# Retention and a routed expert layer: order of the last routing steps, and two weight halves between VectorE and GpSimd

## The chip, the cores and the metric

The kernel runs on one core of a Trainium2 chip. The metric is the device time of one execution in microseconds (us). The kernel before has a median of 381.22 us over 3 runs (381.2 to 381.51).

## The reference

Inputs are `q`, `k`, `v` of shape (4, 8, 768, 64) and an expert layer with a gate of (512, 8), `w1` of (8, 512, 1024) and `w2` of (8, 1024, 512). First comes a retention, a linear attention whose state decays by a factor per head:

```python
for t in range(S):
    state = gamma * state + einsum('bhd,bhe->bhde', k[:, :, t], v[:, :, t])
    y[:, :, t] = scale * einsum('bhd,bhde->bhe', q[:, :, t], state)
```

Its result, as 3072 tokens of 512 features, goes to eight experts. Each token goes to one:

```python
logits = x @ w_gate
expert_idx = argmax(logits, axis=1)
gate_w = softmax(logits)[arange(N), expert_idx]
for e in range(E):
    xe = x[expert_idx == e]
    out[expert_idx == e] = gate_w * (relu(xe @ w1[e]) @ w2[e])
```

## The kernel before, in words

**Retention.** The tokens are worked in 24 chunks of 128 (4 batches of 6 chunks), two chunks per turn of the loop at L606 (n = 0 to 11, `last` = 11). A turn computes scores, the carried state and the output on TensorE. VectorE takes the output out of PSUM (`evict`, L331), TensorE transposes it (`rows`, L340), and ScalarE copies the rows to SBUF. `logits` and `finish_logits` (L378, L387) multiply the same output with the gate.

**Gating.** The chunks fall into seven groups (L47); the last two, 5 and 6, are chunks 20, 21 and chunks 22, 23. A group goes through `choose` (L417, VectorE: maximum, tie-break and one-hot of the expert, seven instructions for a group of two chunks), `soft` (L436, ScalarE: exponentials), `rank` (L439, TensorE: small matmuls that count the tokens of each expert so far), `slots`, `weights`, `advance` (L450, L483, L456, VectorE) and `label` (L487, two copies on ScalarE). Then GpSimd scatters the rows of the chunk into a DRAM area sorted by expert (`send_apart`, L358); between two such sends it has a `pause`, a small operation on one partition (L199).

**The early expert.** Once 18 chunks are ranked, the kernel knows one expert with many rows and loads 256 of its rows (`fetch_early`). In the last turn they are transposed, and split into a high half (ScalarE, `cut_high`) and a low half (`cut_low`: the first 128 rows on GpSimd, the second on VectorE). All products are made of three matmuls: high by high, low by high, high by low. The expert's work is cut into 32 pieces of 6 matmuls (`early_pieces`, L883): two per block of 128 hidden features, two per block of the second product. Order: hidden 0, hidden 1, result 0, hidden 2, result 1, and so on. After the second piece of a hidden block ScalarE applies relu (L904), and VectorE takes the low half of that (L905). `fill(n)` (L547) emits the next n pieces. They fill TensorE between the gating steps of the last two groups; `FILL` (L46) has the counts. `mark_early` (L536) makes the scatter indices of the early rows for later, in four VectorE instructions.

**Weights.** A quarter of an expert's weights is loaded to `raw` (a ring of two buffers, L125) and split by `split` (L140): ScalarE copies the high part, and the engine that is passed subtracts it for the low part. For the first expert this is done in steps of 512 columns, whose turns stand in `SPLITS` (L60); turn 11 has one, the last step of quarter 1. For the second expert a quarter is split in two halves of 1024 columns; its first quarter is split at the end of `late_block` (L1050), which works the early expert's remaining rows ahead of the loop over the experts 1 to 7 (L1119).

**Order.** Everything around the change is under a manual schedule: each engine runs its instructions in the order in which the program emits them. Behind the last choice stands a chain of small VectorE instructions (L733 to L757) that counts the tokens of each expert, sorts the experts by count and computes pad rows; it leads to the loads of the next experts' rows and weights (L761 to L773).

Of the kernel before, what the change touches and what calls it, by code (L numbers as in the profile page):

```python
# [42 lines left out]
ROW = 4 * SLICE  # L43
MAXB = CMAX32 // 32
WARM = 8
FILL = (1, 3, 4)  # L46
GROUPS = ((0, 6), (6, 6), (12, 4), (16, 2), (18, 2), (20, 2), (22, 2))  # L47
FULL = 18
BEHIND = {3: (0, 1), 4: (2, 3), 5: (4, 5), 6: (6, 7), 7: (10, 11), 8: (12, 13)}
# [10 lines left out]
SPLITS = {n: tuple(next(_ORDER) for _ in range(c)) for n, c in _PIECES.items()}  # L60
# [47 lines left out]
def retention_moe(ctx, tc, front, qkv, w1, w2, first_rows, second_rows, out):  # L108
    nc = tc.nc
# [111 lines left out]
    with ExitStack() as actx:  # L221
# [136 lines left out]
        def send_apart(chunks, between=pause):  # L358
            for i, g in enumerate(chunks):
                if i:  # L360
                    between()
                send_rows(g)
# [24 lines left out]
        def finish_logits(t):  # L387
            i = [n for n, (a, w) in enumerate(GROUPS) if a <= 2 * t < a + w][0]
            a, w = GROUPS[i]
            both = ps_1.tile([P, 2, TW], F32, name="lp", tag="misc")  # L390
            lp, state["spare"] = both[:, 0].rearrange("p (c n e) -> p c n e", c=2, n=NP), both[:, 1]
            for ci in range(2):
                nc.tensor.transpose(out=lp[:, ci].rearrange("t p e -> t (p e)"),
                                    in_=state["LT"][:, ci * C:(ci + 1) * C], identity=ident)
            if w == 2:
                lgs[i] = state["spare"][:, 3 * w * E:4 * w * E].rearrange("p (i e) -> p i e", e=E)
            elif 2 * t == a:
                lgs[i] = gsm.tile([P, w, E], F32, name=f"lg{w}")
            nc.vector.tensor_reduce(out=lgs[i][:, 2 * t - a:2 * t - a + 2, :], axis=AX.X, op=ALU.add,
                                    in_=lp[:, :, :, 0:E].rearrange("t c p e -> t c e p"))  # L400
# [131 lines left out]
        def cut_early():  # L532
            for j, w, eng in first["pieces"]:
                cut_low(nc, eng, *first["x"], first["xt"], j, w)

        def mark_early():  # L536
            xg0 = first["xg"]
            index, weight = slot_marks[0]
            empty = gsm.tile([P, NJ0], F32, name="empty0")
            nc.vector.tensor_tensor(out=empty, in0=k_("slot")[:, 0:NJ0], in1=s0.broadcast_to([P, NJ0]), op=ALU.is_ge)  # L540
            nc.vector.tensor_scalar(out=mask0, in0=empty, scalar1=float(BIG), scalar2=k_("quad"),
                                    op0=ALU.mult, op1=ALU.add)
            nc.vector.scalar_tensor_tensor(out=index[:, 0:NJ0], in0=xg0.bitcast(I32)[:, :, P], scalar=4 * ROWS,
                                           in1=mask0, op0=ALU.bitwise_and, op1=ALU.bitwise_or)
            nc.vector.tensor_copy(out=weight[:, 0:NJ0], in_=xg0[:, :, P + 1:P + 2])

        def fill(n):  # L547
            for _ in range(n):
                fn, a = early.pop(0)
                fn(*a)  # L550
# [49 lines left out]
        last = NCH // 2 - 1  # L600
# [5 lines left out]
        for n in range(last + 1):  # L606
            a, b = 2 * n, 2 * n + 1
            s = gating(chosen[n]) if n in chosen else None
            if s:
                stages[chosen[n]] = s  # L610
            begin(n)
            if n == soon:
                logits(n - 1)
            else:
                if n == 0:
                    output(a)
                carry(n)
            if n > 0:
                if n == last:
                    turn_early()  # L620
                if n != soon:
                    logits(n - 1)
                if n == last:
                    for j, w, _ in first["pieces"]:
                        cut_high(nc, first["x"][0], first["xt"], j, w)
                if n in AMID:
                    send_behind(state["LT"][:, 0:1], AMID[n])
                rows(a - 2, "s0")
                rows(a - 1, "s1")
                finish_logits(n - 1)  # L630
            if n in (6, 7):
                for i in SPLITS[n]:
                    split(0, *i, nc.gpsimd if n == 6 else nc.vector, 1)
            if s and n < last:
                s["choose"]()
            if n == soon:
                carry(n)
            if b % CPB < CPB - 1:
                update(b)
            if s and n < last:  # L640
                s["soft"]()
            if n > 0:
                output(a)
            if n == soon:
                s["rank"]()
            output(b)
            if n == soon:
                for name in ("slots", "weights", "label", "counts"):
                    s[name]()
                nc.vector.tensor_copy(out=filled, in_=full)  # L650
                nc.vector.tensor_scalar(out=s0, in0=full, scalar1=base, scalar2=float(EARLY), op0=ALU.subtract,
                                        op1=ALU.min)
                nc.vector.tensor_tensor(out=start, in0=s0, in1=base, op=ALU.add)
                send_apart(range(FULL - 2, FULL))
                fill_late()
                fetch_early()
            elif s and n < last:
                s["rank"]()
                s["slots"]()
            for g in (a, b):  # L660
                evict(g)
            if n == GROUPS[0][1] // 2:
                s["totals"]()
            if n == last:
                cut_early()
                s["choose"]()
            elif s:
                for name in ("weights", "label")[2 * (n == soon):] + ("advance",):
                    s[name]()
            if n == soon - 1:  # L670
                scale(b + 2)
                scale(a + 4)
            if n in BEHIND:
                send_behind(xTs[n][:, 0, C:C + 1], BEHIND[n], pause if n == soon - 1 else lambda: scale(b + 2))
            if n == 1:
                nc.vector.tensor_scalar(out=run, in0=k_("ebase"), scalar1=1.0 / P, scalar2=None, op0=ALU.mult)
            if n < last:
                if n > 0:
                    update(a + 2)
                if n in AFTER:  # L680
                    pause()
                    send_behind(ubs[(a + 2) % 3][:, 0, 0:1], AFTER[n])
                scores(a + 2)
                if n == 0:
                    update(a + 2)
                scores(b + 2)
            if n == GROUPS[0][1] // 2:
                s["pick"]()
                expert_at[0] = nc.sync.value_load(first_at[0:1, 0:1], min_val=0, max_val=E - 1)
                fetch(0, 0)  # L690
                fill_rows()
                fetch(0, 2)
            if n == 0:
                nc.scalar.copy(out=wgs[:, :, 0:E], in_=k_("gates").rearrange("p (k e) -> p k e", k=NP))
            if n < last:
                if n not in BEHIND:
                    scale(b + 2)
                if n < last - 1 and n != soon - 1:
                    scale(a + 4)
            for i in SPLITS.get(n, ()) if n > 7 else ():  # L700
                split(0, *i, nc.gpsimd, 1)
            for g in (a, b):
                if FIRST <= g < NCH - AHEAD - len(MID):
                    load(g + AHEAD + len(MID))
                if g in fetches:
                    fetch(0, fetches[g])
                for i in LATER.get(g, ()):
                    load(i)
        send_apart(range(FULL, FULL + 2))
        mark_early()  # L710

        s = stages[5]
        fill(FILL[0])
        rows(2 * last, "U", ps_1)
        logits(last)
        rows(2 * last + 1, "s1")
        s["soft"]()
        fill(FILL[1])
        s["rank"]()
        for name in ("slots", "weights", "advance", "label"):  # L720
            s[name]()
        send_apart(range(20, 22))
        finish_logits(last)
        final = gating(6)
        final["choose"]()
        fill(FILL[2])
        final["soft"]()
        final["rank"]()
# [42 lines left out]
        expert_at[2] = place(2)  # L771
        for part in range(3):
            fetch(1, part)  # L773
        for i, pieces in enumerate((4, 3, 3, 2)):
            fill(pieces)
            split(0, 3, i, nc.vector, 1)
# [156 lines left out]
def moe_main(ctx, tc, wparts, fetch, split, xhl1, Z0, ident, buf, xg, fetch_rows, expert_at, held7, mask7, slot_marks, natural, overflow,  # L933
             last_meta, pad_regions, token_index, pause, out):
    nc = tc.nc
# [114 lines left out]
    def late_block():  # L1050
# [48 lines left out]
        turned(1)  # L1099
        prep(2, "low")  # L1100
        prep(3, "high", "low")
        for i in range(2):
            split(1, 0, i, nc.vector)
        marks(1)
        for j in range(-(-NJ0 // 4)):
            weigh(0, j)
# [246 lines left out]
```

## Time and profile before

The profiled execution took 381.39 us; its span, from first to last instruction, is 379.6 us.

| engine | busy us | share of the span |
|---|---|---|
| TensorE matmul (PE) | 372.5 | 98% |
| TensorE weight load (PEld) | 350.5 | 92% |
| VectorE (DVE) | 251.9 | 66% |
| ScalarE (ACT) | 140.6 | 37% |
| GpSimd (POOL) | 262.2 | 69% |

Times in the rows are microseconds from the span's start. L12 is line 12 of the kernel; out<-in are the program's names. Matmuls are pipelined and their ends are modelled, so starts are the better measure. Spans on GpSimd are rough. A bracket at the end of a row says how long the engine was idle before it, and what ended that.

### The profile page before, as it was taken

The page shows a single profiled execution, that of the slowest core. Times are in us where ns is not written, and L with a number is a line of the kernel's source. Part 1 is how long each engine was busy: PE and PEld are TensorE (multiplying, and loading weights), DVE is VectorE, ACT ScalarE, POOL GpSimd, SP SyncE. Part 2 cuts the span into 40 slices and gives each one's busy share as a digit, 9 for nine tenths or more (in the row PEclk, how much of TensorE's full clock was granted, in tenths as well). Part 3 has the DMA queues.
Part 4 walks back from the last instruction along what each step waited for, and adds up shares of the span by engine and source line. Part 5 has one row for each costly group of instructions (what it writes and reads, how often), then busy time and mean ns, then how long its engine had stood idle before and what let it go on. Part 6 is the DMA issues. An engine that isn't in the chain of part 4 may idle for free. (4 is left out here: it accounts for less than half of the span.)

```text
span 379.6 us, 8704 instructions
## 1 busy us (share of the span) xinstructions
PE 372.5 (98%) x3279; PEld 350.5 (92%) x3279; DVE 251.9 (66%) x495; ACT 140.6 (37%) x251; POOL 262.2 (69%) x278
## 2 busy tenths in 40 slices
PE   8999999999999999999999999999999999999994
PEld 5888888888899899999999999999999999999984
DVE  3457857887776785967885777576676667676211
ACT  2222244235532645443540553154235316423100
POOL 3751669988770369507996999499669929886874
PEclk9999999999999999999999999999999999999999
DMA  8999999986249579769655654856557557520102
GB/s 303 417 418 416 418 397 419 415 348 167 94 156 190 209 187 298 247 224 253 215 183 104 217 183 142 182 175 194 144 152 221 180 91 239 185 105 17 43 23 77
DMA packets 42030, 82.05 MB, mean 216 GB/s; under 512 B 4267, under 2 KB 17583, under 8 KB 39536
## 3 DMA queue, kind: packets, MB, share of 16 engines
q1 hardware_dynamic: 36656, 67.67, 54.2%
q0 software_dynamic: 5312, 13.49, 9.9%
q8 instruction: 47, 0.77, 0.9%
q14 instruction: 15, 0.12, 0.1%
HBM read 65.80 MB, written 15.82 MB: 215 GB/s over the span
## 5 line engine op out<-in xcount | busy, mean ns | idle before, releaser
L841 POOL DMA_INDIRECT out<-Z,sidx x88 | 101.7, 1156 | 63.8 <-DVE Z L1044 49.1
L146 DVE TENSOR_TENSOR wlo<-raw,whi 128x1024 fp32r<-128x1024 f32 (+1 forms) x63 | 74.2, 1184 | 17.5 <-ACT whi L145 17.4
L201 POOL TENSOR_TENSOR idle<-cs 1x256 bf16<-1x256 f32 x102 | 80.4, 788 | 2.9
L145 ACT CAST whi<-raw 128x1024 fp32r<-128x1024 f32 (+1 forms) x72 | 67.5, 950 | 8.2 <-DMA raw<-w 8.1
L1201 PE MATMUL py<-hh,whi 128*128 128x392 f32 (+4 forms) x192 | 65.9, 343 | 0.0
L1201 PE MATMUL py<-hl,whi 128*128 128x392 f32 (+4 forms) x192 | 65.9, 343 | 0.0
L1201 PE MATMUL py<-hh,wlo 128*128 128x392 f32 (+4 forms) x192 | 65.9, 343 | 0.0
L1176 ACT ACTIVATE hh<-ph 128x452 fp32r<-128x452 f32 (+6 forms) x56 | 28.4, 506 | 73.6 <-PE ph L1169 73.6
L1169 PE MATMUL ph<-xl,whi 128*128 128x392 f32 (+5 forms) x224 | 48.9, 340 | 0.0
L1169 PE MATMUL ph<-xh,wlo 128*128 128x392 f32 (+5 forms) x224 | 48.9, 340 | 0.0
L1169 PE MATMUL ph<-xh,whi 128*128 128x392 f32 (+5 forms) x224 | 48.8, 340 | 0.0
L1177 DVE SCALAR_TENSOR_TENSOR hl<-ph,hh 128x452 fp32r<-128x452 f32 (+6 forms) x56 | 32.0, 573 | 17.5 <-ACT hh L1176 16.8
L1169 PEld LDWEIGHTS ph<-xh,whi 128*128 128x128 f32 x224 | 40.2, 188 | 0.3
L1169 PEld LDWEIGHTS ph<-xl,whi 128*128 128x128 f32 x224 | 40.2, 188 | 0.1
L1169 PEld LDWEIGHTS ph<-xh,wlo 128*128 128x128 f32 x224 | 40.2, 188 | 0.1
L1201 PEld LDWEIGHTS py<-hl,whi 128*128 128x128 f32 x192 | 36.1, 188 | 0.2
L1201 PEld LDWEIGHTS py<-hh,wlo 128*128 128x128 f32 x192 | 36.1, 188 | 0.2
L1201 PEld LDWEIGHTS py<-hh,whi 128*128 128x128 f32 x192 | 36.0, 188 | 0.2
L863 ACT CAST xh<-buf 128x512 fp32r<-128x512 f32 (+7 forms) x26 | 14.4, 556 | 52.6 <-DVE buf L856 52.5
L280 DVE TENSOR_TENSOR Sb<-sp,cs 128x512 f32<-128x512 f32 x48 | 29.8, 682 | 5.8 <-PE sp L277 5.8
L841 POOL DMA_INDIRECT x_sorted<-xrow,KEY x24 | 25.0, 1040 | 7.1 <-issue 3.9
L1039 DVE STREAM_TRANSPOSE Z<-py 128x416 f32<-128x416 f32 (+3 forms) x24 | 15.0, 624 | 18.7 <-PE py L1201 18.4
(197 smaller groups left out, 555.3 us busy)
## 6 DMA issues: line engine op xcount, KB each, us to landing
raw<-w SPq DMA_DIRECT2D x32, 1024.0 KB, 6.7
qkv_w<-qkv SPq DMA_DIRECT2D x12, 1024.0 KB, 17.5
qkv_t<-qkv SPq DMA_DIRECT2D x7, 1024.0 KB, 16.4
qkv_t<-front SPq DMA_DIRECT2D x7, 512.0 KB, 6.9
buf<-x_sorted SPq DMA_DIRECT2D x12, 211.2 KB, 5.2
x_sorted<-cs SPq DMA_DIRECT2D x7, 260.0 KB, 6.5
buf<-x_sorted SPq DMA_DIRECT2D x8, 195.0 KB, 3.8
out<-Z,sidx POOLq DMA_INDIRECT x88, 2.5
```

The costliest lines, as they stand in the source:

```text
L145: nc.scalar.copy(out=hi[:, h], in_=raw[:, h])
L146: engine.tensor_tensor(out=lo[:, h], in0=raw[:, h], in1=hi[:, h].bitcast(F32), op=ALU.subtract)
L201: nc.gpsimd.tensor_tensor(out=idle[0:1], in0=cs[0:1, 0:PAUSE], in1=cs[0:1, 0:PAUSE], op=ALU.mult)
L280: nc.vector.tensor_tensor(out=Sb[:, r], in0=sps[r], in1=causal.unsqueeze(1).broadcast_to([P, NP, C]), op=ALU.mult)
L841: sc = tc.nc.gpsimd.indirect_dma_start(out=dst, out_offset=bass.IndirectOffsetOnAxis(ap=index, axis=0), in_=rows, in_offset=None, bounds_c ...
L863: nc.scalar.copy(out=xh[:, :, c0:c0 + w], in_=xt[:, :, t0:t0 + w])
L1039: nc.vector.transpose(out=Zs[e][:, 0:nb, k, :], in_=py[:, 0:32 * nb].rearrange("p (j c) -> p j c", c=32))
L1169: nc.tensor.matmul(out=ph[:, :w], lhsT=wparts[e, f // 4][a][:, kd, fo:fo + P], rhs=x[:, kd, :w], start=(n == 0), stop=(n == 3 * KD - 1))
L1176: nc.scalar.activation(out=hh[:, :cap], in_=ph[:, :cap], func=AF.Relu)
L1177: nc.vector.scalar_tensor_tensor(out=hl[:, :cap], in0=ph[:, :cap], scalar=0.0, in1=hh[:, :cap].bitcast(F32), op0=ALU.max, op1=ALU.subtract)
L1201: nc.tensor.matmul(out=py[:, :c], lhsT=a[:, f % 4, k * P:(k + 1) * P], rhs=x[:, :c], **se)
```

## The change

It has five parts. In the last turn of the loop, group 5's `choose` is emitted ahead of the early rows' low half. Group 5's `rank` comes ahead of the second early piece, `label` ahead of `advance`, and `FILL` becomes (1, 1, 2): one piece instead of three lies between the last rows and the last logits' transposes, and two instead of four ahead of the last rank. The four pieces left over are emitted later, behind the loads of the second expert's weights, and `mark_early` moves there too. The weight step of turn 11 goes from GpSimd to VectorE, behind the last `choose`. In `late_block`, the second half of the second expert's first quarter goes from VectorE to GpSimd.

```diff
-FILL = (1, 3, 4)
+FILL = (1, 1, 2)
...
             if n == last:
+                s["choose"]()
                 cut_early()
-                s["choose"]()
...
-            for i in SPLITS.get(n, ()) if n > 7 else ():
+            for i in SPLITS.get(n, ()) if 7 < n < last else ():
                 split(0, *i, nc.gpsimd, 1)
...
         send_apart(range(FULL, FULL + 2))
-        mark_early()
 
         s = stages[5]
         fill(FILL[0])
...
         logits(last)
         rows(2 * last + 1, "s1")
         s["soft"]()
-        fill(FILL[1])
         s["rank"]()
-        for name in ("slots", "weights", "advance", "label"):
+        for name in ("slots", "weights", "label", "advance"):
             s[name]()
         send_apart(range(20, 22))
+        fill(FILL[1])
         finish_logits(last)
         final = gating(6)
         final["choose"]()
+        for i in SPLITS[last]:
+            split(0, *i, nc.vector, 1)
         fill(FILL[2])
         final["soft"]()
         final["rank"]()
...
         for part in range(3):
             fetch(1, part)
+        fill(4)
+        mark_early()
         for i, pieces in enumerate((4, 3, 3, 2)):
             fill(pieces)
             split(0, 3, i, nc.vector, 1)
...
         prep(3, "high", "low")
-        for i in range(2):
-            split(1, 0, i, nc.vector)
+        for i, eng in enumerate((nc.vector, nc.gpsimd)):
+            split(1, 0, i, eng)
         marks(1)
```

## Rows read from the trace of the kernel before

**Rows 1.** Busy time by stretch: PE, PEld, DVE, ACT, POOL; clock; DMA share, GB/s.

```profile
86.00:372.00 286.00, 285.97 (x1797) 278.16 (x1796) 194.53 (x347) 112.57 (x180) 203.51 (x207) 1.00 0.56 167
...
160.00:170.00 10.00, 10.00 (x54) 9.81 (x53) 7.47 (x11) 4.43 (x6) 0.00 (x0) 1.00 0.65 216
```

**Rows 2.** Timeline of TensorE's matmuls: start, us, line, out<-in, count.

```profile
99.05 0.48 PE L896 MATMUL ph<-xh,wlo 128*128 128x256 f32 x2
...
99.83 0.64 PE L896 MATMUL ph<-xh,whi 128*128 128x256 f32 x4
...
101.26 0.18 PE L441 MATMUL pf<-EA,us 128*128 128x16 bf16 x1
...
101.48 0.42 PE L393 MATMUL lp<-cs,LT 128*128 128x128 f32 x2
...
104.54 0.18 PE L441 MATMUL pf<-EA,us 128*128 128x16 bf16 x1
...
134.78 0.92 PE L1169 MATMUL ph<-xh,wlo 128*128 128x420 f32 x4
```

**Rows 3.** Timeline of VectorE.

```profile
97.83 1.27 DVE L870 TENSOR_TENSOR xl<-xt,xh 128x512 fp32r<-128x512 f32 x1
99.03 0.16 DVE L422 TENSOR_REDUCE mx<-lp 128x2 f32<-128x16 f32 x1
...
100.03 0.61 DVE L540 TENSOR_TENSOR empty<-cs,s 128x8 f32<-128x8 f32 x1
...
101.10 0.42 DVE L905 SCALAR_TENSOR_TENSOR hl<-ph,hh 128x256 fp32r<-128x256 f32 x1
101.88 0.42 DVE L905 SCALAR_TENSOR_TENSOR hl<-ph,hh 128x256 fp32r<-128x256 f32 x1 [0.35 <-ACT hh L904]
102.22 0.17 DVE L452 TENSOR_TENSOR rk<-pf,EA 128x16 f32<-128x16 f32 x1
...
102.50 0.16 DVE L484 TENSOR_REDUCE GW<-exs 128x2 f32<-128x18 f32 x1
...
102.85 0.22 DVE L399 TENSOR_REDUCE lp<-lp 128x16 f32<-128x64 f32 x1
...
104.04 0.16 DVE L434 TENSOR_TENSOR sh<-lp,mx 128x16 f32<-128x16 f32 x1
...
105.49 0.17 DVE L452 TENSOR_TENSOR rk<-pf,EA 128x16 f32<-128x16 f32 x1
...
109.83 0.23 DVE L371 TENSOR_SCALAR pads<-ends,cs 128x7 int32<-128x7 f32 x1
...
132.20 2.35 DVE L146 TENSOR_TENSOR wlo<-raw,whi 128x1024 fp32r<-128x1024 f32 x2
...
138.03 1.23 DVE L146 TENSOR_TENSOR wlo<-raw,whi 128x1024 fp32r<-128x1024 f32 x1 [0.31 <-ACT whi L145]
```

**Rows 4.** Timeline of GpSimd.

```profile
97.27 1.29 POOL L146 TENSOR_TENSOR wlo<-raw,whi 128x512 fp32r<-128x512 f32 x1
...
124.14 0.60 POOL L201 TENSOR_TENSOR idle<-cs 1x256 bf16<-1x256 f32 x1
...
138.64 1.07 POOL L201 TENSOR_TENSOR idle<-cs 1x256 bf16<-1x256 f32 x1
```

**Rows 5.** Timeline of ScalarE.

```profile
99.33 0.59 ACT L348 COPY xrow<-tr 128x512 f32<-128x512 f32 x1
100.15 0.22 ACT L437 ACTIVATE exs<-sh 128x16 f32<-128x16 f32 x1 [0.23 <-DVE sh L434]
...
101.46 0.38 ACT L904 ACTIVATE hh<-ph 128x256 fp32r<-128x256 f32 x1 [0.82 <-PE ph L896]
102.90 0.21 ACT L490 COPY xrow<-GW 128x8 f32<-128x8 f32 x1 [1.05 <-DVE GW L485]
...
131.02 2.00 ACT L145 CAST whi<-raw 128x1024 fp32r<-128x1024 f32 x2
```

**Rows 6.** Timeline of TensorE's weight loads.

```profile
134.59 0.76 PEld L1169 LDWEIGHTS ph<-xh,wlo 128*128 128x128 f32 x4
```

## The prediction

> **What bounds the kernel now.** I read the busy shares of the page first, then a table of stretches, then the timelines of the engines around the edit. From 86 to 372 us TensorE is busy for 285.97 of 286.00 us at a granted clock of 1.00; VectorE has 194.53 us of work there, ScalarE 112.57 and GpSimd 203.51 [rows 1]. All edits lie inside this stretch. Nobody else's idle time matters: TensorE does the same matmuls before and after, so a microsecond saved on VectorE buys nothing, and a microsecond for which TensorE must wait is a microsecond of the total. The ends of matmuls are modelled, so I go by starts: six 128x256 matmuls take 0.7 us, two pieces of the early expert 1.43 us (99.83 to 101.26), and no start is late [rows 2]. The question is only where the new order leaves TensorE without operands.
>
> **Choice ahead of the low half, and where group 5 is ranked.** The choice of rows 20 and 21 moves in front of the early rows' low half: it runs from 99.03 to 100.03 now, 1.00 us, and would start at 97.83 [rows 3]. The low half then starts at 98.83. It took 1.27 us, beside GpSimd's weight half of 97.27 (1.29 us) [rows 3, 4]. That half is leaving GpSimd, so I take 0.7 us: VectorE's 128x1024 subtractions take 2.35 us for two [rows 3], 0.6 us per 512 columns. It ends at 99.5 instead of 99.10; the 0.60 us pause between two row sends [rows 4] can push that to 100.1. TensorE ranks group 5 at 99.05, behind the transposes, and the choice is ready by 98.83: no wait. The rank takes 0.22 us (101.26 to 101.48), so the second half of hidden block 0, which needs the low rows from its third matmul on (about 99.6), may wait up to 0.5 us, likely 0.1. It takes 0.78 us (99.05 to 99.83) [rows 2].
>
> **Fewer pieces between lp and the last rank: the main term.** Before, four pieces lie between the transposes of the last logits and the last rank: 101.48 to 104.54, 3.06 us [rows 2]. After, there are two, 1.43 us. Without waits TensorE would reach the last rank at 99.05 + 0.22 + 0.78 + 0.20 (the two transposes: 3.06 less 2 x 1.43) + 1.43 + 0.08 for the first of a group = 101.75 us.
>
> What that rank needs comes later, because both other queues are in program order. ScalarE copies the last rows' transposes until 99.92, then takes exp (0.22 us) to about 100.1 [rows 5]. VectorE then does the weights; the label follows 0.40 us after they start (102.50 to 102.90) [rows 3, 5], so at 100.5. In the new order the label stands ahead of the relu of block 0: two copies 0.1 us apart, and relu runs 100.70 to 101.08 (0.38 us). VectorE's low half of that relu follows 0.04 us later, as 101.88 follows 101.46 + 0.38, and the next instruction 0.34 us after it starts: 101.46 [rows 3, 5]. Only there comes the reduce of the last logits and the last choice: 102.85 to 104.20 before, 1.35 us, so until 102.81 after; with the hand-over 102.85. TensorE would stand from 101.75 to 102.85: **1.1 us**. Bounds: if the low half of the relu didn't hold VectorE, the reduce would follow the transposes at 100.4 and the rank could start at 101.8, a wait of 0.1; with the late low rows everything shifts by 0.4, a wait of 1.5. I take the middle value since each link of it has its own row.
>
> **The weight half moved to VectorE** stands behind the last choice. It costs VectorE about 0.65 us after 102.8, ahead of the low half of block 1, which the second result block needs only about 3 us after the rank. TensorE's cost is 0. It delays the release of its raw buffer to about 103.5, and the load into that buffer stands behind the order of experts, which comes out of VectorE's long chain (105.49 to 109.83 before) [rows 3]. Cost 0; without that cover it would be the 5 us by which the release is late.
>
> **mark_early moved** takes its four instructions (100.03 to 101.10, 1.07 us [rows 3]) from ahead of the gating to behind the pad chain. There they stand between the low halves of blocks 2 and 3. The gating and the chain run about 1.7 us earlier (slots at 103.8 instead of 105.49, pads done at 108.4 instead of 110.06), so block 2's low half is there at 108.8; TensorE wants it 0.26 + 4 x 1.43 = 6.0 us after the rank, at 108.9, and block 3's almost 3 us later. Cost 0, with 0.1 us to spare; if the chain loses more to the pauses, up to 0.4. Scatters of the last rows, pads and loads of rows go out about 1.5 us earlier; since TensorE has no wait for them to shorten [rows 1], they give 0.
>
> **The half of the next expert moved to GpSimd: the second term.** ScalarE has both high halves at 133.02 (131.02 + 2.00) [rows 5]. VectorE does its half from 132.20 to 133.38 [rows 3]. A GpSimd operation that meets one of VectorE's with both inputs in SBUF waits for it: the pause at 138.64 takes 1.07 us beside VectorE's subtraction of 138.03 to 139.26, against 0.60 us alone [rows 3, 4]; in the same way the low half of 97.83 waited for GpSimd. So GpSimd starts in effect at 133.38. Its time for 128x1024 is not in the trace; twice its 128x512 is 2.58 us, VectorE's own is 1.18. By the nearest row, its own, it ends at 135.96. TensorE loads the third of four low weights at 134.59 + 2 x 0.19 = 134.97 [rows 6], for the group that starts at 134.78 [rows 2]. That is 0.99 us late by the full double, 0.8 if half of a fixed share is saved, and nothing at VectorE's speed. I take **0.9 us**, bounds 0 to 1.0. All before it in this block hangs on TensorE's own transposes, so the first wait doesn't widen the slack.
>
> The Trainium skill speaks against this edit: "GPSIMD Engine Reference", section 4.1, sends two-input elementwise work to VectorE, being about twice as slow on GpSimd, and section 3.1 has the ratio 1.96. As an estimate from that page, 1.96 x 1.18 = 2.3 us, the half would end at 135.7 and the wait be 0.7 us. Section 8 names the shared SBUF interfaces with contention for two SBUF inputs, and the trace agrees (1.07 against 0.60 us).
>
> What queues behind this half: the weighing of the first expert's rows on VectorE, which has both inputs in SBUF, starts some 2 us later, and so do the nine scatters behind it; VectorE has room in the next blocks, and GpSimd is empty from 160 to 170 us [rows 1]. The loads of weights behind it start 1.4 us later; they cost 0 while ScalarE is not held beyond its slack.
>
> **Sum.** 1.1 + 0.9 = 2.0 us on the profiled execution's 381.39 us (span 379.6, and 1.8 around it) = 383.4. That run lies 0.17 us above the median of 381.22, so **383.2 us**.
>
> **Rivals.**
> Only one of the two waits comes: GpSimd finishes in time because its 1024 columns cost well under two times 512, or the last choice gets through. For: no row has that size on GpSimd. Against: it has 1.6 us from 133.38 for what would be 2.3 to 2.6. Time 381.22 + 0.9 to 1.1 = 382.2. Chance 0.17.
>
> Not slower: the choice of the last group isn't held. Its place is ScalarE's queue: if relu of block 0 got in ahead of the label, or if the last choice ended by 101.75, the 1.1 us go; with GpSimd done by 134.97, nothing is left. It decides at the start of the last logits' reduce: by 100.4 there is no wait. For: the gating chain as a whole runs 1.7 us earlier. Against: program order on ScalarE and VectorE. Time 381.2 to 381.7. Chance 0.16.
>
> Faster: group changes on TensorE cost about 0.08 us more than the steady pace; if modelled ends hide waits there, five changes give back 0.4, and low rows or pads that come earlier might end one that I can't see. 380.8 or below; against it stands 285.97 of 286.00 [rows 1]. Chance 0.06.
>
> Worse: the long chain loses to pauses, block 2's low half is late too, and weights of the next expert are held up behind the later loads: 0.4 + 0.5 more, 384.1. Chance 0.06.
>
> **How the numbers follow.** My forecast, with both waits, has 0.55; its own range is 382.6 to 383.8. Slower by over 0.2% (0.76 us, about what this kernel's measurement can tell from no change) takes the forecast, the single wait and the worse case: 0.78. Within 0.2% takes the not-slower rival and a small share of the faster one, 0.16; faster is 0.06. The range 381.4 to 383.9 leaves out most of the cases without a wait and the worst one.
>
> **What would show it.** TensorE's table of waits, nearly empty in this stretch now, would have a wait of about 1.1 us at the last rank for VectorE, around 102 us, and one of about 0.9 us at the first hidden block of the second expert for GpSimd, near 136 us; the reduce of the last logits would start near 101.5, and one GpSimd subtraction of 128x1024 would take 2.3 to 2.6 us. A start of the last rank below 102.2 us, or that GpSimd half under 1.7 us, would break a term. TensorE busy without a gap would make the whole wrong.

## The result, and the profile after

The changed kernel takes 384.14 us (median of 7 runs, 383.48 to 385.65) against 381.42 us for the kernel before on the same chip (381.2 to 382.56): a ratio of 1.0066 (95% interval 1.0053 to 1.0079), slower by 2.7 us where 2.0 were forecast, and 0.24 us above the range (381.4 to 383.9). The profiled execution took 384.24 us, 2.85 more than the one before (381.39). The granted clock has no part in it: it is 1.00 in every stretch below, as before.

The windows of the changed kernel answer to [rows 1] (columns as there, two shorter stretches added):

```profile
86.00:374.00 288.00, 286.87 (x1795) 277.78 (x1793) 196.16 (x347) 112.92 (x180) 205.91 (x207) 1.00 0.56 166
...
95.00:105.00 10.00, 9.30 (x108) 8.03 (x103) 7.22 (x31) 5.14 (x15) 8.94 (x9) 1.00 0.32 121
...
134.00:144.00 10.00, 9.56 (x50) 8.83 (x49) 9.57 (x11) 3.93 (x7) 8.43 (x7) 1.00 0.63 159
```

TensorE now has gaps in two stretches that the change touches: 0.70 us in 95 to 105 us and 0.44 us in 134 to 144 us. Its table of waits from 90 to 140 us (us in total, times, longest) names one releaser for each:

```profile
PE pf L441 <- DVE sh L434: 0.7, 1, 0.7
PE ph L1172 <- POOL wlo L146: 0.4, 1, 0.4
```

Matmul ends are modelled, so these entries are smaller than what is lost from start to start. TensorE's timeline, which answers to [rows 2]:

```profile
99.20 0.17 PE L441 MATMUL pf<-EA,us 128*128 128x16 bf16 x1
...
99.40 0.48 PE L899 MATMUL ph<-xh,wlo 128*128 128x256 f32 x2
99.89 0.71 PE L899 MATMUL ph<-xl,whi 128*128 128x256 f32 x4
100.44 0.38 PE L393 MATMUL lp<-cs,LT 128*128 128x128 f32 x2
100.57 0.72 PE L899 MATMUL ph<-xh,whi 128*128 128x256 f32 x4
...
101.61 0.64 PE L899 MATMUL ph<-xl,whi 128*128 128x256 f32 x4
102.91 0.18 PE L441 MATMUL pf<-EA,us 128*128 128x16 bf16 x1 [0.66 <-DVE sh L434]
...
109.11 0.30 PE L922 MATMUL acc<-hl,whi 128*128 128x256 f32 x1
...
136.97 0.65 PE L1172 MATMUL ph<-xh,wlo 128*128 128x420 f32 x2 [0.44 <-POOL wlo L146]
...
376.89 0.28 PE L1020 MATMUL py<-whi,hl 128*104 128x256 f32 x1
```

Four matmuls of the early expert take 0.48 us from start to start (101.13 to 101.61), so the last rank could have started at 101.61 + 0.48 = 102.09. It started at 102.91, 0.82 us later. Another 0.26 us was lost just before: the two matmuls at 99.40 kept TensorE 0.49 us instead of the 0.32 of [rows 2] (99.05 to 99.37 before), and the four at 99.89, the first to use the low rows, took 0.55 instead of 0.46 (99.37 to 99.83 before). The low rows end at 99.74 on VectorE. That is 1.08 us in this stretch. VectorE's timeline shows why, and answers to [rows 3]:

```profile
98.92 0.82 DVE L873 TENSOR_TENSOR xl<-xt,xh 128x512 fp32r<-128x512 f32 x1
...
101.15 0.42 DVE L908 SCALAR_TENSOR_TENSOR hl<-ph,hh 128x256 fp32r<-128x256 f32 x1 [0.58 <-ACT hh L907]
101.49 0.22 DVE L399 TENSOR_REDUCE lp<-lp 128x16 f32<-128x64 f32 x1
...
102.69 0.16 DVE L434 TENSOR_TENSOR sh<-lp,mx 128x16 f32<-128x16 f32 x1
102.77 0.68 DVE L146 TENSOR_TENSOR wlo<-raw,whi 128x512 fp32r<-128x512 f32 x1
...
103.70 0.17 DVE L452 TENSOR_TENSOR rk<-pf,EA 128x16 f32<-128x16 f32 x1
...
108.41 0.23 DVE L371 TENSOR_SCALAR pads<-ends,cs 128x7 int32<-128x7 f32 x1
108.55 0.42 DVE L908 SCALAR_TENSOR_TENSOR hl<-ph,hh 128x256 fp32r<-128x256 f32 x1
...
133.44 1.22 DVE L146 TENSOR_TENSOR wlo<-raw,whi 128x1024 fp32r<-128x1024 f32 x1
134.58 2.37 DVE L982 SCALAR_TENSOR_TENSOR sidx<-buf,empty 128x15 int32<-128x15 int32 x1
```

The low half of block 0 (101.15) stands ahead of the last logits' reduce (101.49), as forecast at 101.46, and the last choice ends at 102.85. GpSimd's timeline, answering to [rows 4], and the row of ScalarE that releases the half, answering to [rows 5]:

```profile
134.35 2.57 POOL L146 TENSOR_TENSOR wlo<-raw,whi 128x1024 fp32r<-128x1024 f32 x1 [9.99 <-ACT whi L145]
...
378.00 1.01 POOL L844 DMA_INDIRECT out<-yo,pair  x1 [1.62 <-DVE yo L1026]
```

```profile
132.26 2.00 ACT L145 CAST whi<-raw 128x1024 fp32r<-128x1024 f32 x2
```

The half started when ScalarE's second high half was there (134.26), took 2.57 us and ended at 136.92; TensorE's third low weight starts right behind it. From one matmul's start to the next pass 0.79 us there (136.18 to 136.97), where the steady pace is 0.19: 0.60 us late, and 0.66 us by the end of the block.

**Where the 2.85 us are.** The last matmul starts at 376.89 instead of 374.55: 2.34 us. Of these 1.08 are the stretch of the last rank, 0.66 the GpSimd half, 0.10 a low half of rows near 124 us, 0.07 the start of the program, and 0.20 and 0.21 two short stops of TensorE, at 159 and 195.6 us, for which the table of waits names no other engine:

```profile
158.94 0.19 PEld L1204 LDWEIGHTS py<-hh,whi 128*128 128x128 f32 x1 [0.27 <-issue]
...
195.59 0.19 PEld L1204 LDWEIGHTS py<-hh,whi 128*128 128x128 f32 x1 [0.30 <-issue]
```

"issue" means that the engine waited for nothing that the view shows. The trace's single records, which include the branch instructions that the views leave out, show TensorE's own queue at work there: it reads an expert's row count into a register (L962) and branches on it (L970). The branch begins at 158.83 and at 195.48, and the weight load follows 0.11 us later in both. What made the queue late at these two places is not shown. The other 0.51 us come after the last matmul: from its start to the end of the execution pass 7.35 us instead of 6.84 (384.24 − 376.89; 381.39 − 374.55). The kernel before has these rows there, its last matmul and its last scatter:

```profile
374.55 0.28 PE L1017 MATMUL py<-whi,hl 128*104 128x256 f32 x1
```

```profile
375.66 1.01 POOL L841 DMA_INDIRECT out<-yo,pair  x1 [1.61 <-DVE yo L1023]
```

### The profile page after: what moved, and what is told of

The parts are those of the page before. It is cut to its first block, busy times and chain, and to the rows that moved or that the text cites. A ratio compares the mean times of both kernels' runs of the same rounds, so it can differ in the third digit from the quotient of the medians.

```text
span 382.5 us, 8706 instructions
## 1 busy us (share of the span) xinstructions
PE 373.8 (98%) x3279; PEld 350.6 (92%) x3279; DVE 253.5 (66%) x495; ACT 140.9 (37%) x251; POOL 264.9 (69%) x278
## 5 line engine op out<-in xcount | busy, mean ns | idle before, releaser
L844 POOL DMA_INDIRECT out<-Z,sidx x88 | 105.0, 1194 | 54.3 <-DVE Z L1047 39.6
L201 POOL TENSOR_TENSOR idle<-cs 1x256 bf16<-1x256 f32 x102 | 78.0, 765 | 2.8
```

The source lines that it names most:

```text
L201: nc.gpsimd.tensor_tensor(out=idle[0:1], in0=cs[0:1, 0:PAUSE], in1=cs[0:1, 0:PAUSE], op=ALU.mult)
L844: sc = tc.nc.gpsimd.indirect_dma_start(out=dst, out_offset=bass.IndirectOffsetOnAxis(ap=index, axis=0), in_=rows, in_offset=None, bounds_c ...
```

## The experiments

Each run stands beside the kernel before on the same chip. "End" is, in the profiled execution, the span less the start of the last matmul: 5.05 us before (379.6 − 374.55), 5.61 us after (382.5 − 376.89). Spans are rounded to 0.1 us, so ends are good to 0.05 us.

| run | median us | before | ratio (95%) | end us |
|---|---|---|---|---|
| e1 half on VectorE | 383.11 | 381.47 | 1.0047 (1.0034 to 1.0060) | 5.59 |
| e2 GpSimd half alone | 382.62 | 381.47 | 1.0045 (1.0027 to 1.0062) | 5.55 |
| e3 pieces before the rank | 384.12 | 381.47 | 1.0067 (1.0054 to 1.0080) | 5.55 |
| e4 e1 and e3 | 383.16 | 381.47 | 1.0047 (1.0034 to 1.0060) | 5.52 |
| e5 choice first | 382.76 | 381.57 | 1.0033 (1.0021 to 1.0044) | 5.60 |
| e6 before again | 381.41 | 381.57 | 0.9996 (0.9988 to 1.0005) | 5.13 |
| e7 quarter on GpSimd | 382.56 | 381.57 | 1.0029 (1.0019 to 1.0039) | 5.61 |
| e8 six pieces | 382.65 | 381.57 | 1.0026 (1.0016 to 1.0035) | 5.54 |
| e9 e5, step on GpSimd | 381.79 | 381.51 | 1.0007 (0.9993 to 1.0021) | 5.11 |
| e10 e8, mark_early in front | 382.39 | 381.51 | 1.0029 (1.0018 to 1.0039) | 5.54 |
| e11 after again | 384.18 | 381.51 | 1.0074 (1.0059 to 1.0089) | 5.59 |
| e12 before, two swapped | 381.36 | 381.51 | 1.0000 (0.9990 to 1.0011) | 5.09 |

### The two halves of the loss: e1 and e2

e1 is the changed kernel with the next expert's half back on VectorE; e2 is the kernel before with that half alone on GpSimd (its diff is this one read the other way).

```diff
-        for i, eng in enumerate((nc.vector, nc.gpsimd)):
-            split(1, 0, i, eng)
+        for i in range(2):
+            split(1, 0, i, nc.vector)
```

> The changed kernel with both halves of the second expert's first quarter on VectorE again. Theory (TensorE's two waits add up, 1.1 us at the last rank and 0.66 us behind GpSimd's half): the wait near 136 us goes, the one near 102 us stays, 0.7 us less than the changed kernel, some 383.5 us where that has 384.1. Rival (what GpSimd's half delays behind it, the weighing, the scatters and the weight loads, costs as much again): 1.2 to 1.6 us less, 382.6 to 382.9 us.

> The kernel before with GpSimd's half as the only edit. Theory: one TensorE wait of about 0.7 us at the third low weight of the second expert, 0.7 us slower than before, 382.1 us. Rival (later loads and scatters cost as well): 1.2 to 1.6 us slower, 382.6 to 383.0 us. If TensorE is not the bound in this stretch at all: the same time as before.

Each kept one wait of the table and lost the other. The whole tables of waits of e1 and of e2, from 90 to 140 us:

```profile
PE pf L441 <- DVE sh L434: 0.7, 1, 0.7
```

```profile
PE ph L1169 <- POOL wlo L146: 0.4, 1, 0.4
```

e1 is 1.64 us slower than before on the median, e2 1.15. So GpSimd's wait belongs to the moved half, and the rank's wait to the other four parts together. But both also have the longer end: 1.64 is about 1.08 and 0.5, 1.15 about 0.66 and 0.5. The sum of both, 2.79, counts the end twice, and the changed kernel is 2.72 slower; about 0.4 us is left by this subtraction, as much as the short stops of the profiled execution.

### Is it the number of pieces ahead of the last rank? e3 and e4

```diff
-FILL = (1, 1, 2)
+FILL = (1, 1, 4)
...
-        fill(4)
+        fill(2)
         mark_early()
```

e4 has this and the half on VectorE.

> The changed kernel with four pieces again between the last logits' transposes and the last rank (counts 1, 1, 4, and two pieces fewer behind it). Theory: two pieces are 1.43 us of matmuls, more than the 1.1 us wait, so the last rank waits for nothing and the kernel is 1.1 us faster than the changed one, 383.0 us. Rival (the wait is put off: the low halves of later blocks or the pad chain come late instead): under 0.4 us faster, and a new wait between 103 and 112 us.

> The changed kernel with both: four pieces ahead of the last rank, and both halves on VectorE. The choice ahead of the low half, group 5 ranked early, mark_early late and the weight step on VectorE stay. Theory: no wait of TensorE is left, within 0.4 us of the kernel before, 381.2 to 381.8 us. Rival (0.5 us or more of the loss lies in none of the two waits but in the parts that stay, or in a changed end of the program): 0.5 to 0.9 us slower than before.

My theory missed and the rival held: no gain. The rank's wait went, as two pieces more cover it, but another came, in e3 (0.6 in its table of waits) as in e4. e3's profiled execution has two further stops, of about 1.0 us from 182 to 185 us and 0.7 at 196.6 us, which e4's has not, so e4's rows are shown. TensorE's and VectorE's timelines in e4:

```profile
107.94 0.28 PE L922 MATMUL acc<-hh,wlo 128*128 128x256 f32 x1
108.81 0.39 PE L922 MATMUL acc<-hl,whi 128*128 128x256 f32 x1 [0.59 <-DVE hl L908]
```

```profile
103.65 0.17 DVE L452 TENSOR_TENSOR rk<-pf,EA 128x16 f32<-128x16 f32 x1
...
108.19 0.23 DVE L371 TENSOR_SCALAR pads<-ends,cs 128x7 int32<-128x7 f32 x1
108.33 0.42 DVE L908 SCALAR_TENSOR_TENSOR hl<-ph,hh 128x256 fp32r<-128x256 f32 x1
```

The slots start at 103.65 (103.70 in the changed kernel), so block 2's low half, behind the pad chain, starts at 108.33 (108.55 there), whether TensorE waited before or not. With two or with four pieces ahead of the rank, VectorE decides when TensorE goes on: its line runs from the last choice through the weight step (0.68 us), block 1's low half and the slots to the pads. In the changed kernel TensorE used that low half at 109.11, so the 0.82 us at the rank had paid for this wait already.

### Shortening VectorE's line: e5 and e9

e5 is e1 with the last logits' transposes and the last choice ahead of block 0's second piece, and the weight step behind the pieces.

```diff
-FILL = (1, 1, 2)
+FILL = (1, 0, 3)
...
         final["choose"]()
+        fill(FILL[2])
         for i in SPLITS[last]:
             split(0, *i, nc.vector, 1)
-        fill(FILL[2])
```

e9 is e5 with that weight step on GpSimd, as before the change:

```diff
-            for i in SPLITS.get(n, ()) if 7 < n < last else ():
+            for i in SPLITS.get(n, ()) if n > 7 else ():
                 split(0, *i, nc.gpsimd, 1)
...
-        for i in SPLITS[last]:
-            split(0, *i, nc.vector, 1)
```

> Both halves on VectorE, and the last logits' transposes and the last choice emitted ahead of the second half of hidden block 0, so that no relu stands in front of them on VectorE; the weight step of turn 11 behind the two blocks. Theory (VectorE's line from the last choice through the pad chain to the low half of block 2 is what TensorE waits for, at the last rank or at the second result block): the reduce of the last logits starts near 100.5 instead of 101.2, the whole line 0.7 to 0.9 us earlier, both waits gone or under 0.2 us; 1.0 us faster than the version with both halves on VectorE (383.1), 382.1 us. Rival (the line is held by something ahead of it, the low rows or the weights of group 5): under 0.4 us gained.

> The version with the choice first (both halves on VectorE), and the weight step of turn 11 back on GpSimd where the kernel before has it. There the last rank waited for nothing, yet the low half of block 2 ended at 108.6 and TensorE waited 0.55 us for it, because VectorE had the 0.69 us step between the choice and the slots. Theory (VectorE's line is the bound between the last choice and block 2's low half): the line ends 0.5 to 0.6 us earlier, near 108.0, TensorE waits under 0.1 us anywhere from 99 to 122 us; 0.5 us less than that version, 382.2 us. Rival (the pauses on GpSimd, not the step, set the line): under 0.2 us gained.

e5's VectorE timeline with the matmul that waits, and e9's VectorE timeline:

```profile
100.40 0.22 DVE L399 TENSOR_REDUCE lp<-lp 128x16 f32<-128x64 f32 x1
...
102.88 0.69 DVE L146 TENSOR_TENSOR wlo<-raw,whi 128x512 fp32r<-128x512 f32 x1
103.49 0.17 DVE L452 TENSOR_TENSOR rk<-pf,EA 128x16 f32<-128x16 f32 x1
...
108.17 0.42 DVE L908 SCALAR_TENSOR_TENSOR hl<-ph,hh 128x256 fp32r<-128x256 f32 x1
```

```profile
108.64 0.38 PE L922 MATMUL acc<-hl,whi 128*128 128x256 f32 x1 [0.39 <-DVE hl L908]
```

```profile
103.11 0.16 DVE L452 TENSOR_TENSOR rk<-pf,EA 128x16 f32<-128x16 f32 x1
...
107.97 0.42 DVE L906 SCALAR_TENSOR_TENSOR hl<-ph,hh 128x256 fp32r<-128x256 f32 x1
```

In e5 the last reduce starts at 100.40 instead of 101.49 and the rank has no wait. But the low halves of blocks 0 and 1 and the 0.69 us step then fill VectorE until the slots at 103.49, and TensorE waits 0.55 us for block 2's low half (0.4 in the table of waits). Without the step, in e9, the slots start 0.85 us behind the start of the last rank (102.26) instead of 1.67 in e5 (101.82), the table is empty from 90 to 140 us, and the time can't be told from before. e9 gains about 0.9 us over e5, as its end is short again too. So the step that the forecast put at nothing costs 0.55 us once the rank no longer waits; it was hidden in the changed kernel by the rank's own wait.

### What mark_early costs: e8 and e10

e8 is e1 with all six pieces ahead of the last rank; e10 has mark_early ahead of the gating again as well.

```diff
-FILL = (1, 1, 2)
+FILL = (1, 1, 6)
...
-        fill(4)
         mark_early()
```

```diff
         send_apart(range(FULL, FULL + 2))
+        mark_early()
...
-        mark_early()
```

> Both halves on VectorE, six pieces ahead of the last rank (hidden 1, result 0, hidden 2), none ahead of mark_early, so that the low half of block 2 stands ahead of the pad chain as in the kernel before. Theory: no TensorE wait between 99 and 122 us; 382.0 us, before plus the 0.5 us at the end. Rival (mark_early and the weight step behind or inside the chain still delay a low half, now block 3's): a wait of 0.3 us or more at the third result block, 382.4 us or above.

> The version with six pieces ahead of the last rank, and mark_early back in front of the gating. There TensorE waited 0.45 us at the third result block for block 3's low half, which stood behind the pad chain and mark_early. Theory: without the 1.07 us the low half is ready at 110.5 and TensorE waits for nothing; 0.4 to 0.5 us less, 382.2 us, which is before plus the 0.5 us at the program's end. Rival (the pad chain alone makes it late): the wait stays, 382.6 us.

VectorE in e8, and the matmul that waits:

```profile
109.89 0.23 DVE L371 TENSOR_SCALAR pads<-ends,cs 128x7 int32<-128x7 f32 x1
110.03 0.58 DVE L540 TENSOR_TENSOR empty<-cs,s 128x8 f32<-128x8 f32 x1
...
111.07 0.42 DVE L907 SCALAR_TENSOR_TENSOR hl<-ph,hh 128x256 fp32r<-128x256 f32 x1
```

```profile
111.54 0.39 PE L921 MATMUL acc<-hl,whi 128*128 128x256 f32 x1 [0.27 <-DVE hl L907]
```

With no pieces between chain and mark_early, its 1.04 us (110.03 to 111.07) hold back block 3's low half, and TensorE waits there (0.3 in the table of waits). In e10 that low half starts at 109.92 and the table of waits is empty, yet the kernel is still 0.9 us slower than before: 0.5 is the end. Its profiled execution (382.10 us) starts the last matmul 0.21 us later than before (374.76 against 374.55), and that comes from the early rows' low half, as in the changed kernel: it ends at 99.58, the first matmul that uses it starts at 99.73, and 0.27 us are lost there from start to start, of which the table of waits names nothing.

### A shorter GpSimd step, and the end of the program: e7, e6, e11, e12

e7 is the kernel before with 512 columns on GpSimd instead of 1024:

```diff
-        for i in range(2):
-            split(1, 0, i, nc.vector)
+        split(1, 0, 0, nc.vector)
+        for i, eng in ((2, nc.vector), (3, nc.gpsimd)):
+            split(1, 0, i, eng, 1)
```

e6 and e11 have no edit (the kernel before, the changed kernel). e12 swaps two independent instructions of mark_early in the kernel before:

```diff
+            nc.vector.tensor_copy(out=weight[:, 0:NJ0], ...)
             nc.vector.scalar_tensor_tensor(out=index[:, 0:NJ0], ...)
-            nc.vector.tensor_copy(out=weight[:, 0:NJ0], ...)
```

> The kernel before, with only the last 512 of the 2048 columns of the second expert's first quarter on GpSimd, the rest on VectorE. Theory (the wait is GpSimd's time for 1024 columns, 2.57 us, against what TensorE needs): 1.29 us from about 133.1 end at 134.4, ahead of the fourth low weight at 135.16: no wait of TensorE, and only the 0.5 us at the end of the program that the variants have, 381.5 to 382.0 us. Rival (any GpSimd operation there, sharing SBUF with VectorE, delays the block): a wait of 0.3 us or more at the first hidden block.

> The kernel before, unchanged, in another execution: how much of the 0.5 us that the changed kernel and four variants have between their last matmul and their end (5.57 us, 5.05 before) belongs to the program and not to the execution. If to the program: the end is 5.05 us again and the time equals before within 0.1%. If to the execution: some other value, with no tie to the order of the work.

> The changed kernel, unchanged, in another execution. Theory: the two waits (0.9 to 1.0 us at the last rank, 0.6 us behind GpSimd's half) and the end of 5.57 us come again, within 0.1 us; the two small delays of 0.2 us at result matmuls near 159 and 195 us, which no engine released, need not: they should differ in place or size. Rival: they come again in the same places, and then belong to the program as well.

> The kernel before with two independent VectorE instructions of mark_early in the other order, no work added or taken. If the 0.5 us at the end follows from how the program comes to lie, and not from the change's work, any variant may have it: 5.57 us from the last matmul to the end and 382.0 us. If it follows from the change: 5.07 us as before and 381.5 us.

GpSimd's step in e2 and in e7:

```profile
132.88 2.58 POOL L146 TENSOR_TENSOR wlo<-raw,whi 128x1024 fp32r<-128x1024 f32 x1 [7.22 <-ACT whi L145]
```

```profile
133.06 1.39 POOL L146 TENSOR_TENSOR wlo<-raw,whi 128x512 fp32r<-128x512 f32 x1 [7.12 <-ACT whi L145]
```

The shorter step ends at 134.45, and no wait for it is in TensorE's table: the half was too long, the quarter isn't. Yet e7 is 1.0 us slower than before, about half of it the end; its profiled execution lost another 0.24 us at the matmul that stopped at 159 us in the changed kernel. The end isn't chance of one execution: before, e6, e12 and e9 have 5.05 to 5.13 us, and the ten other executions have 5.52 to 5.61. These ten all have a weight subtraction moved to or from GpSimd; the four others have GpSimd's subtractions as before. Reordering VectorE alone (e12) or moving the choice and the pieces (e9) doesn't do it. That is a correlation only: GpSimd's last scatter stands as near to the last matmul in the changed kernel (1.11 us: 378.00 − 376.89) as in the kernel before (375.66 − 374.55), so the time goes after it.

The trace's single records show where. Behind the last scatter SyncE runs the program's closing instructions, which the views don't count as busy, and two of them (DRAIN) stand one behind the other. In the four short ends the second starts 0.06 us after the first and takes 0.01; in all ten long ends it starts 0.36 us after the first and takes 0.13, and GpSimd's next closing instruction starts 4.79 to 4.81 us after the last matmul's start instead of 4.30 to 4.32. So the 0.5 us are one stop of SyncE, of the same size in every such execution. Why these builds have it stays open.

e11 repeats the changed kernel's waits (0.7 and 0.4 us), but it lost hardly anything at 159 and 195 us. It lost 0.33 us near 123.7 instead, where the changed kernel's first execution lost 0.10: TensorE goes on there behind a low half of rows that took VectorE 1.08 us, against 0.88 in that execution and 0.69 before. So the size of these losses depends on the execution; the places recur, as e7 has the stop of 159 us and e3 that of 195.6.

## Why the prediction was right and wrong

**Right: direction and mechanism.** Both waits came where forecast, with the releasers forecast. Taking back the GpSimd half removed its wait (e1), and taking back the other four parts removed the rank's (e2).

**Right: the last rank, 1.1 us.** Measured 1.08. The chain of the forecast (label ahead of relu, relu's low half ahead of the last reduce) is there: reduce forecast at 101.46 and measured at 101.49, rank at 102.85 and at 102.91. Of the 1.08, the late low rows took 0.26 (forecast: likely 0.1) and the rank itself 0.82; as VectorE sets the rank's start, the first only eats from the second.

**Mis-sized: the GpSimd half, 0.9 us; measured 0.66.** Its price was right (two times 128x512 is 2.58 us, measured 2.57), its start was not: I let it begin in effect when VectorE's half ends. It began at 134.35, right behind ScalarE's second high half (134.26), while VectorE's half ran until 134.66, and took no longer for it. In the times of the kernel before, where ScalarE is done 1.24 us sooner (133.02), that start is 133.11 instead of the forecast's 133.38, 0.27 us earlier, which takes the full double's 0.99 us of lateness to 0.72. By the Trainium skill, "GPSIMD Engine Reference", section 3.1, a two-input add of 2048 columns takes 1.96 times as long as on VectorE; here, for 1024 columns, it is 2.57 to 1.22 us, 2.1 times. The forecast's estimate from that page, a wait of 0.7 us, came close by two errors that cancel: 2.3 us is too short, and the start it counts from is 0.27 us late. The half fits the full double that I took the upper bound from.

**Wrong: the sum.** This is the step that failed. It put 2.0 us "on the profiled execution's 381.39 us (span 379.6, and 1.8 around it)" and so put at nothing, without a row for it, whatever else could change. The part behind the last matmul grew by 0.51 us, by the stop of SyncE, and 0.58 us of small delays came along the way (0.07 at the start, 0.10 at a low half of rows, 0.41 at two branches of TensorE's queue). 1.08 + 0.66 + 0.58 + 0.51 is 2.83 of the 2.85 measured. The rule of the forecast, that only TensorE's waits for operands count, is what failed: the end lies behind TensorE's work, and a stop at a branch is no wait for operands. The 0.24 us too much for the GpSimd half hid part of this, which was luck. Another 0.20 us of the distance is no fault of the sum: the kernel before has 381.42 us beside the changed one, and the forecast started from 381.22.

**Costs put at nothing.** The weight step on VectorE and mark_early cost nothing that shows in the changed kernel, as forecast. For the step this was so only as the rank's wait covered it: e5 and e9 give 0.55 us for it. For mark_early it was so only as four pieces stood ahead of it: e8 and e10 show it holding back block 3 without them. The "0.1 to spare" for block 2 was close (low half done at 108.97, used at 109.11), and it is the next bound. What queues behind GpSimd's half came as forecast (first scatter of marked rows at 138.33 instead of 135.60); no wait on TensorE followed that the trace names.

**The rivals.** "Only one of the two waits" and "faster" are refuted by the table of waits. "Worse", 384.1 us, came nearest in time but not by its mechanism: block 2's low half was not late in the changed kernel, only in e3, e4 and e5. "Not slower" named its deciding point well: in e5 the reduce starts at 100.40, where the forecast wanted 100.4 or earlier, and the rank has no wait; that this only moves the wait to block 2 was not foreseen.

No version beat the kernel before; e9 can't be told from it.

## What to carry to other kernels

Where TensorE had no gap, ordering work earlier on another engine bought nothing (e9), and each piece of cover taken away must be checked against the other engine's own program order: what stands ahead of the reduce on VectorE set the loss here, not the length of the choice. A wait that is removed shows the next one on the same line (rank, block 2, block 3), so cut work from the line (e9) before shifting cover along it (e3, e5, e8). And allow for a part outside the accounted stretch, here 0.5 us: repeat the unchanged kernel and read the end of the program, down to its closing instructions, before calling a small remainder a wait.

## What the runs showed of the hardware

A VectorE operation of 15 columns with two SBUF inputs lasted 2.37 us (134.58 to 136.95) beside GpSimd's subtraction, which ended at 136.92, so VectorE's line stood still until then; e2 has the same 2.37 us. In the kernel before, with GpSimd idle, it took 0.17 us:

```profile
134.47 0.17 DVE L979 SCALAR_TENSOR_TENSOR sidx<-buf,empty 128x15 int32<-128x15 int32 x1
```

The Trainium skill, "GPSIMD Engine Reference", section 8, names the contention, and the trace agrees. The other way round GpSimd's 2.57 us (twice its 128x512 is 2.58) was no longer for VectorE's operation that ran for its first 0.31 us; starts on GpSimd are rough.

The end of the program differed by 0.5 us between builds whose last scatters are alike, by one stop between two closing instructions of SyncE (0.36 us from the start of one to the next instead of 0.06), with a moved GpSimd subtraction as the only thing in common. TensorE stopped by some 0.2 us (0.7 in e3) where its queue branches on a row count, in some executions. The cause of both stays open.
